# Regrouping the MLP tiles of an attention-plus-MLP kernel from 2,2,2,4,4,4,4,2 to 2,2,2,2,4,4,4,4, with the planner settings that go with it

## Chip, cores and metric

The kernel runs on one core of one Trainium2 chip. The metric is the device time of one execution in microseconds, the median over several. All times inside an execution are counted from the start of its profiled span. Engines carry the profile's names: PE (TensorE), DVE (VectorE), ACT (ScalarE), POOL (GpSimd), and SP (SyncE), which only issues transfers.

## What is computed

Windowed attention with four sink positions, followed by a two-layer MLP on the normalised result, with a residual. Cut to the essentials:

```python
# q, k, v: 4 batches x 8 heads x 768 positions x 64, float32; n_sink = 4, window = 128
scores = (q @ k.T) / 8
keep = (pos_k < 4) | ((0 <= pos_q - pos_k) & (pos_q - pos_k < 128))
a = softmax(where(keep, scores, -1e9)); attn = a @ v
x = attn.transpose(0, 2, 1, 3).reshape(4, 768, 512)
xn = (x - mean(x)) / sqrt(var(x) + 1e-6) * g_ln
out = x + relu(xn @ w_ch1) @ w_ch2          # 512 -> 2048 -> 512
```

## The kernel before, in words

**Tiles.** The 4 x 768 positions are 24 tiles of 128, numbered t = 6b + r (batch b, r from 0 to 5). A tile passes through these steps on PE:

- *scores* (function `scores`, line 625): eight matmuls of 64 rows, into two wide PSUM buffers. ACT takes the exponential (line 643). DVE (line 653; line 647 where r = 0) or POOL (lines 655 and 658) applies the window mask.
- *values* (function `values`, lines 713 and 716): the weighted sums of tile t use scores of tile t and of tile t - 1, and so come after the scores of t. For r of 2 and more there are also two sink matmuls (line 696). `normalise` follows on DVE: reciprocals and scaling (lines 752 and 753), statistics (765, 768), centring to `xn` (773).
- the *turn* of the centred tile into `xnt`, either on PE (line 812, copied back by ACT or DVE) or by a DMA transpose that SP issues (line 802) where t is in `BY_DMA`.
- *up* (line 836) and *down* (line 876). One `up` step fills one PSUM bank with 512 columns: for a group of four tiles it is 4 matmuls of 512 columns, for a group of two 8 of 256. `down` is 16 matmuls of 512 columns for a tile, then DVE's line 889, then SP's store (line 894).

**Groups.** `GROUPS` says how many consecutive tiles share an `up`. An up needs the turned `xnt` of *all* tiles of its group. The reciprocal standard deviation of a group is two POOL instructions (lines 785 and 787), emitted once for the group when its last tile's statistics exist.

**Sinks.** Per batch, `sinks` scores all queries against four keys (line 570). For batches 1 and 2 it is two parts: tiles of r = 2 and 3, then of r = 4 and 5. For the others it is one part over r = 2 to 5, so that it needs the transposed queries of four row blocks at once. A batch in `JOINED` has its first part appended behind the scores of its r = 2 tile.

**Values and scores.** Unless t - 1 is in `ALONE` (or t = 6), the values of tile t - 1 and the scores of tile t are one planned unit, in which the sink matmuls run on 64 rows for each half; a tile in `ALONE` has its values planned by themselves, with sink matmuls of 128 rows.

**Transfers.** For batches 1 to 3, POOL issues the loads: q and k blocks (line 409, into a ring of six `qb` buffers), v blocks (418), first rows of v (449). SP issues a DMA transpose for each `qb` (line 508) into `qkt`; when it has landed, its `qb` is free for the load six places later. POOL and SP take their instructions strictly in order, and so POOL's lines 785/787 and 655/658 stand in one queue with the loads, and SP's stores and turns in one queue with the transposes of q and k.

**Order.** `Plan.emit` is a list scheduler that runs when the kernel is built. Each operation has modelled costs, a due key, and dependences. A tile's attention key is `up_pos` of its group minus `LEAD` (30.0) minus 6.9 for each tile that follows it in the group. `up_pos` and `down_pos` count MLP work in the order `mlp_order`: ups of the first `NB0` = 3 groups, their downs, then up and down of each further group. DMA transposes carry a modelled extra latency, the last argument of `op`. The order is fixed in the program; on the chip each engine runs its list and waits where it must.

Of the kernel before, what the change touches and what calls it, by code (L numbers as in the profile page):

```python
# [38 lines left out]
class Plan:  # L39
# [18 lines left out]
    def op(self, engs, fn, deps=(), key=0.0, alloc=(), uses=(), lat=0.0):  # L58
        o = Op(engs, fn, deps, key, alloc, uses)
        o.lat = lat  # L60
        self.ops.append(o)
        return o
# [108 lines left out]
def kernel(  # L171
# [22 lines left out]
    NT = B * RB  # L194
# [4 lines left out]
    assert NS == 4 and W == 128 and D == 64 and S == 768 and DM == H * D  # L199


    GROUPS = [2, 2, 2, 4, 4, 4, 4, 2]
    JOINED = (3,)
    QB = 6
    ALONE = (6, 7, 8, 9)
    NB0 = 3
    NG = len(GROUPS)
    FIRST = [sum(GROUPS[:g]) for g in range(NG)]
    assert sum(GROUPS) == NT
    where = {FIRST[g] + i: (g, i) for g in range(NG) for i in range(GROUPS[g])}  # L210

# [19 lines left out]
    def copy(e, dst, src):  # L231
        if e == "ACT":
            nc.scalar.copy(dst, src)  # L233
        else:
            ENG[e].tensor_copy(dst, src)
# [7 lines left out]
    def room_for(buf):  # L243
        return wide[buf.slot // 2] if buf.pool == "pw" else single[buf.slot - 4]
# [5 lines left out]
    op = plan.op  # L250
# [4 lines left out]
    for s, g in mlp_order:  # L255
        (up_pos if s == "u" else down_pos)[g] = pos
        pos += 3.46 * GROUPS[g]
    LEAD = 30.0
    NEG_TILES = 3
    BY_DMA = [t for t in range(10, NT) if t != 13]  # L260
    W2_FIRST = 3

    def akey(t):
        g, ti = where[t]
        if g < NB0:
            return t - 100.0
        return up_pos[g] - LEAD - 6.9 * (GROUPS[g] - 1 - ti)

# [134 lines left out]
    def load_qk(b, x, r, key, deps=()):  # L403

        qb = Buf("qb", QB)

        def go(_):
            qb.t = qbp.tile([128, H * D], BF16, name="qb")
            nc.gpsimd.dma_start(qb.t.rearrange("p (h d) -> p h d", h=H),  # L409
                                (q, k)[x][b, :, 128 * r:128 * (r + 1), :].rearrange("h p d -> p h d"))  # L410

        prep(b, x, r, load(0.9, 0.9, go, key, deps, [qb]), key, qb)
# [43 lines left out]
    prepped, kqb, turns = {}, {}, {}  # L456

    def qkt_buf(b):
        if b in kqb:
            return []  # L460
        kqb[b] = Buf("qkt", 2)
        return [kqb[b]]
# [37 lines left out]
    def prep(b, x, r, lo, key, qb):  # L500

        alloc = qkt_buf(b)
        kb = kqb[b]

        def go(_):
            if kb.t is None:
                kb.t = qkt.tile([128, 2, HP, S], BF16, name="qkt")
            nc.sync.dma_start_transpose(kb.t[:, x, :, 128 * r:128 * (r + 1)], qb.t)  # L508

        o = op({"SP": 1.25}, go, [lo], key, alloc, [kb, qb])  # L510
        prepped[(b, r, x)] = op({"DMA": 0.75}, None, [o], key, (), [kb, qb], 0.8)

    def ready(b, hps, klo, khi, qlo, qhi):

# [165 lines left out]
    xb, xnb, xtb, mvb, rsb, turned = {}, {}, {}, {}, {}, {}  # L680
    aggr = {}

    def values(t, key, joined=False, narrow=False):
# [50 lines left out]
        if joined:  # L734
            return Joined(mm, deps, banks, uses, cost, lambda o: normalise(t, key, o, banks, sums))
        normalise(t, key, op({"PE": cost}, mm, deps, key, banks, uses), banks, sums)

    def normalise(t, key, o, banks, sums):

        b, r = divmod(t, RB)  # L740
        g, ti = where[t]
        vread[(b, r)] = o

        rc = {}

        def recip(_):
            xb[t].t = xpool.tile([128, H, D], BF16, name="xt")
            if len(banks) == 2:
                for half in range(2):
                    pv = sums[half].rearrange("p (h d) -> p h d", d=D + 1)  # L750
                    rc[half] = small.tile([128, 4], FP32, name=f"rc{half}")
                    nc.vector.reciprocal(rc[half], pv[:, :, D])  # L752
                    nc.vector.tensor_tensor(xb[t].t[:, 4 * half:4 * half + 4], pv[:, :, 0:D],  # L753
                                            rc[half].unsqueeze(2).to_broadcast([128, 4, D]), op=ALU.mult)
                return
            pv = room_for(banks[0])[:, :, 0:4 * (D + 1)].rearrange("p a (h d) -> p a h d", d=D + 1)
            rc[0] = small.tile([128, 2, 4], FP32, name="rc")
            nc.vector.reciprocal(rc[0], pv[:, :, :, D])
            nc.vector.tensor_tensor(xb[t].t.rearrange("p (a h) d -> p a h d", a=2), pv[:, :, :, 0:D],
                                    rc[0].unsqueeze(3).to_broadcast([128, 2, 4, D]), op=ALU.mult)  # L760

        def stat(_):
            xf = xb[t].t.rearrange("p h d -> p (h d)")
            st = small.tile([128, 6], FP32, name="st")
            nc.vector.bn_stats(st, xf)  # L765
            if g not in mvb:
                mvb[g] = small.tile([128, 4, 2], FP32, name="mv")
            nc.vector.bn_aggr(mvb[g][:, ti, :], st)

        def cen(_):  # L770
            xf = xb[t].t.rearrange("p h d -> p (h d)")
            xnb[t].t = xnpool.tile([128, DM], BF16, name="xn")
            nc.vector.scalar_tensor_tensor(xnb[t].t, in0=xf, scalar=mvb[g][:, ti, 0:1], in1=gb,  # L773
                                           op0=ALU.subtract, op1=ALU.mult)

        o = op({"DVE": 0.92 if len(banks) == 1 else 1.22}, recip, [o], key, [xb[t]], banks)
        o = op({"DVE": 0.9}, stat, [o], key, (), [xb[t]])
        aggr[t] = o
        o = op({"DVE": 0.75}, cen, [o, gb_done], key, [xnb[t]], [xb[t]])

        n = GROUPS[g]
        if ti == n - 1:
            def power(_):
                ve = small.tile([128, 4], FP32, name="ve")
                nc.gpsimd.tensor_scalar_add(ve[:, 0:n], mvb[g][:, 0:n, 1], 1e-6)
                rsb[g] = small.tile([128, 4], FP32, name="rs")
                nc.gpsimd.tensor_tensor(rsb[g][:, 0:n], ve[:, 0:n], neg_half[:, 0:n], op=ALU.pow)

            rs_done[g] = op({"POOL": 1.0}, power, [sinks_done] + [aggr[t - i] for i in range(n)], up_pos[g] + 15)

        alloc = []
        if ti == 0:
            xtb[g] = Buf("xnt", 3)
            alloc.append(xtb[g])

        def room():
            if xtb[g].t is None:
                xtb[g].t = xtpool.tile([128, NDM, 512], BF16, name="xnt")
            return xtb[g].t[:, :, 128 * ti:128 * (ti + 1)]

        if t in BY_DMA:
            o = op({"SP": 1.25}, lambda _: nc.sync.dma_start_transpose(room(), xnb[t].t), [o], key if t >= 10 else -50, alloc,
                   [xnb[t], xtb[g]])
            turned[t] = op({"DMA": 0.75}, None, [o], key, (), [xnb[t], xtb[g]], 1.0)
            return
        pt = Buf("pm", 0)

        def tr(_):
            room()
            pt.t = room_for(pt).bitcast(BF16)  # L810
            for j in range(NDM):
                nc.tensor.transpose(pt.t[:, 128 * j:128 * (j + 1)], xnb[t].t[:, 128 * j:128 * (j + 1)], ident)  # L812

        def back(e):
            copy(e, room(), pt.t[:, 0:512].rearrange("p (j c) -> p j c", j=NDM))

        o = op({"PE": 0.24}, tr, [o], key, alloc + [pt], [xnb[t], xtb[g]])
        turned[t] = op({"DVE": 0.69, "ACT": 0.59}, back, [o], key, (), [pt, xtb[g]])
# [84 lines left out]
    def attention(t, key):  # L903

        alone = t - 1 in ALONE
        trail = None
        if t % RB == 2:
            if t // RB in JOINED:
                trail = sinks(t // RB, key, True)
# [39 lines left out]
    for b in range(B):  # L949
# [34 lines left out]
        for r in range(RB):  # L984
            if b == B - 2:

                t = RB * (b + 1) + r
# [65 lines left out]
```

## Time and profile before

| | |
|---|---|
| median of 6 runs | 224.11 us (223.18 to 225.5) |
| profiled execution, device time | 223.18 us |
| its span, first to last instruction | 221.4 us |
| PE busy / weight loads busy | 213.9 us (97%) / 121.0 us (55%) |
| DVE, ACT, POOL busy | 115.1, 110.2, 92.0 us |
| granted PE clock | 1.00 throughout |
| PE waits in the span that the waits view names from 47 to 135 us | 1.3 us for `qkt` transposes, 1.0 us for a POOL mask |
| median time from issue to landing, 80 to 134 us | v 8.7, q 8.1, k 7.5, `qkt` transposes 7.8, `xnt` transposes 7.0 us |
| the same, 134 us to the end | `xnt` transposes 2.4, stores 2.0 us |

The profiled execution is the fastest of the six runs, 0.93 us below their median, and its device time is 1.78 us over its span. Matmuls overlap one another in the records, so that the busy share of PE says little about waits; the distance between the starts of successive matmuls does. The median time to landing shows two regimes: while the loads of batches 1 to 3 are under way a transfer lands 7 to 9 us after its issue, afterwards some 2 us after it.

### The profile page before, as it was taken

What the parts mean: (1) busy time and instruction counts of PE and PEld (TensorE: products, weight loads), DVE (VectorE), ACT (ScalarE), POOL (GpSimd) and SP (SyncE); (2) the same over time, 40 slices, a digit from 0 to 9 for tenths busy, and PEclk for the clock granted to TensorE, in tenths of its full rate; (3) what the DMA queues carried; (4) which work ended last, traced back from release to release, by engine and by line L of the source; (5) the groups of instructions that cost most, each with busy time, mean ns of one, the idle gap of its engine ahead of it and who ended that gap; (6) DMA issues with size and microseconds to landing.
All of it is one profiled execution on the core that took longest, in us unless ns stands there. A gap on an engine that the chain in (4) does not pass through costs nothing.

```text
span 221.4 us, 4388 instructions
## 1 busy us (share of the span) xinstructions
PE 213.9 (97%) x1728; PEld 121.0 (55%) x1728; DVE 115.1 (52%) x247; ACT 110.2 (50%) x159; POOL 92.0 (42%) x126
## 2 busy tenths in 40 slices
PE   7999999999989999999989999999999999999994
PEld 7465889874545554445535445544454544444853
DVE  5566867205888984486878675470017660021011
ACT  3679775555555187841376754066703266400620
POOL 8995634867625589469384621120005020000000
PEclk9999999999999999999999999999999999999999
DMA  6999999999999999999999992311011230012102
GB/s 165 169 192 199 190 207 188 117 154 193 165 146 241 161 209 155 132 156 178 136 196 173 144 168 74 118 47 24 4 47 47 71 87 11 0 51 94 47 0 95
DMA packets 104421, 27.41 MB, mean 124 GB/s; under 512 B 96081, under 2 KB 101457, under 8 KB 104402
## 3 DMA queue, kind: packets, MB, share of 16 engines
q0 software_dynamic: 73056, 13.64, 81.9%
q1 hardware_dynamic: 30802, 13.12, 30.8%
q10 hardware_dynamic: 544, 0.39, 0.5%
q8 instruction: 13, 0.21, 0.4%
q14 instruction: 6, 0.05, 0.1%
HBM read 28.05 MB, written 6.29 MB: 155 GB/s over the span
## 4 chain that ended last, share of the span: by engine, by line
PE 48%; DMA 32%; POOL 9%; issue 4%; ACT 3%; DVE 2%; SPq 1%; POOLq 0%; DVEq 0%
PE single L876 23%; PE single L836 20%; DMA qkt<-qb 10%; DMA w2s<-in_moe_w_ch_dram 7%; DMA qb<-in_k_dram 5%; DMA qb<-in_q_dram 4%; DMA qkn<-in_k_dram 3%; DMA vn<-in_v_dram 3%; POOL qb L409 2%; POOL qkn L371 2%; ACT e L643 2%; PE wide L625 2%; POOL vn L418 1%; SPq L508 1%; PE single L713 1%
## 5 line engine op out<-in xcount | busy, mean ns | idle before, releaser
L836 PE MATMUL single<-xnt,w1s 128*128 128x256 bf16 (+1 forms) x512 | 86.9, 326 | 0.0
L836 PEld LDWEIGHTS <-w1s 128*128 128x128 bf16 x512 | 48.9, 98 | 33.6 <-issue 1.7
L643 ACT ACTIVATE e<-wide 128x1024 bf16<-128x1024 f32 x44 | 43.8, 1024 | 43.7 <-PE wide L625 43.5
L876 PE MATMUL single<-w2s,h1t 128*128 128x512 bf16 x256 | 57.5, 379 | 0.0
L889 DVE SCALAR_TENSOR_TENSOR ot<-single,rs,xt 128x512 f32<-128x512 f32 (+2 forms) x25 | 18.2, 729 | 64.0 <-PE single L876 63.5
L845 ACT ACTIVATE h1t<-single 128x512 bf16<-128x512 f32 x60 | 35.8, 597 | 17.3 <-PE single L836 15.9
L876 PEld LDWEIGHTS <-h1t 128*128 128x128 bf16 x256 | 24.4, 98 | 29.6 <-issue 1.3
L876 PE MATMUL single<-w2s,h1n 128*128 128x512 bf16 (+2 forms) x144 | 29.5, 356 | 0.0
L845 ACT ACTIVATE h1n<-single 128x512 bf16<-128x512 f32 x30 | 17.9, 597 | 23.0 <-PE single L836 23.0
L409 POOL DMA_DIRECT2D qb<-in_k_dram x18 | 16.1, 897 | 16.3 <-DMA qkt<-qb 15.1
L418 POOL DMA_DIRECT2D vn<-in_v_dram x24 | 21.4, 899 | 2.6 <-DMA w2s<-in_moe_w_ch_dram 1.6
L409 POOL DMA_DIRECT2D qb<-in_q_dram x18 | 15.9, 884 | 13.4 <-DMA qkt<-qb 6.1
L655 POOL TENSOR_SCALAR_AFFINE_SELECT e<-e 128x512 bf16<-128x512 bf16 x6 | 4.1, 688 | 38.3 <-ACT e L643 38.3
L876 PEld LDWEIGHTS <-h1n 128*128 128x128 bf16 x144 | 12.9, 98 | 12.6 <-issue 0.4
L653 DVE TENSOR_TENSOR e<-e,mask 128x1024 bf16<-128x1024 bf16 x26 | 17.4, 683 | 3.8 <-ACT e L643 3.5
L773 DVE SCALAR_TENSOR_TENSOR xn<-xt,mv,gb 128x512 bf16<-128x512 bf16 x24 | 18.2, 758 | 0.6
L765 DVE BATCH_NORM_STATS2 st<-xt 128x6 f32<-128x512 bf16 x24 | 16.5, 689 | 0.4
L752 DVE RECIPROCAL rc<-single 128x4 f32<-128x4 f32 x34 | 6.0, 177 | 18.9 <-PE single L696 8.5
L713 PEld LDWEIGHTS <-e 128*128 128x128 bf16 x192 | 13.0, 98 | 3.8 <-POOL e L655 1.5
L753 DVE TENSOR_TENSOR xt<-single,rc 128x256 bf16<-128x256 f32 x34 | 14.4, 424 | 1.2
L625 PE MATMUL wide<-qkt 64*128 64x256 bf16 (+1 forms) x192 | 14.4, 262 | 0.1
L233 ACT COPY xnt<-single 128x512 bf16<-128x512 bf16 x9 | 5.3, 590 | 12.8 <-PE single L812 12.8
(69 smaller groups left out, 166.1 us busy)
## 6 DMA issues: line engine op xcount, KB each, us to landing
out_dram<-ot SPq DMA_DIRECT2D x23, 256.0 KB, 2.7
vn<-in_v_dram POOLq DMA_DIRECT2D x24, 128.0 KB, 7.7
qb<-in_q_dram POOLq DMA_DIRECT2D x18, 128.0 KB, 6.6
qb<-in_k_dram POOLq DMA_DIRECT2D x18, 128.0 KB, 6.3
w1s<-in_moe_w_ch_dram POOLq DMA_DIRECT2D x4, 512.0 KB, 11.0
w2s<-in_moe_w_ch_dram POOLq DMA_DIRECT2D x4, 512.0 KB, 14.5
qkn<-in_q_dram POOLq DMA_DIRECT2D x3, 192.0 KB, 4.8
qkn<-in_k_dram POOLq DMA_DIRECT2D x3, 192.0 KB, 5.2
```

The costliest lines, as they stand in the source:

```text
L409: nc.gpsimd.dma_start(qb.t.rearrange("p (h d) -> p h d", h=H), (q, k)[x][b, :, 128 * r:128 * (r + 1), :].rearrange("h p d -> p h d"))
L418: nc.gpsimd.dma_start(vn_buf[b % 2][:, r, :, 0:D], v[b, :, 128 * r:128 * (r + 1), :].rearrange("h p d -> p h d"))
L625: nc.tensor.matmul(pb.t[:, h2, i], lhsT=kb.t[64 * h2:64 * (h2 + 1), 1, hp, 128 * r:128 * (r + 1)], rhs=kb.t[64 * h2:64 * (h2 + 1), 0, hp, ...
L643: nc.scalar.activation(eb.t, pb.t, AF.Exp, scale=scale)
L653: nc.vector.tensor_tensor(ev, ev, mask1[:, 0:n].unsqueeze(1).to_broadcast([128, m, n]), op=ALU.mult)
L713: nc.tensor.matmul(pv[:, hh, :], lhsT=weights_of(t, half, i, h2, 0), rhs=vn[:, r, h, 0:D + 1], start=fresh and hh == 0, stop=(r == 0), ski ...
L765: nc.vector.bn_stats(st, xf)
L773: nc.vector.scalar_tensor_tensor(xnb[t].t, in0=xf, scalar=mvb[g][:, ti, 0:1], in1=gb, op0=ALU.subtract, op1=ALU.mult)
L836: nc.tensor.matmul(pb.t[:, n * i:n * (i + 1)], lhsT=w1s[:, j, 128 * (h0 + i):128 * (h0 + i + 1)], rhs=xtb[g].t[:, j, 0:n], start=(j == 0), ...
L845: nc.scalar.activation(hb.t, pb.t, AF.Relu)
L876: nc.tensor.matmul(pb.t[:, 0:n], lhsT=hidden(g, ht, ti), rhs=w2s[:, ht, c0:c1], start=(ht == 0), stop=(ht == NH1 - 1))
L889: nc.vector.scalar_tensor_tensor(ob.t[:, 0:n], in0=pb.t[:, 0:n], scalar=rsb[g][:, ti:ti + 1], in1=xb[t].t.rearrange("p h d -> p (h d)")[:, ...
```

## The change

The last small group moves to the front, so that groups of two hold tiles 0 to 7 and groups of four hold tiles 8 to 23. Only tiles 6 and 7 keep values planned by themselves. The sinks of batch 3 are no longer appended to scores. Tiles 8 and 9 are turned by DMA and tiles 10 and 11 on PE; tile 13 is turned by DMA as well, so that `BY_DMA` has 14 tiles for 13. The modelled latency of both kinds of DMA transposes is 1.5 us where it was 0.8 and 1.0.

```diff
-    GROUPS = [2, 2, 2, 4, 4, 4, 4, 2]
-    JOINED = (3,)
+    GROUPS = [2, 2, 2, 2, 4, 4, 4, 4]
+    JOINED = ()
     QB = 6
-    ALONE = (6, 7, 8, 9)
+    ALONE = (6, 7)
     NB0 = 3
...
-    BY_DMA = [t for t in range(10, NT) if t != 13]
+    BY_DMA = [8, 9] + list(range(12, NT))
...
-        prepped[(b, r, x)] = op({"DMA": 0.75}, None, [o], key, (), [kb, qb], 0.8)
+        prepped[(b, r, x)] = op({"DMA": 0.75}, None, [o], key, (), [kb, qb], 1.5)
...
-            turned[t] = op({"DMA": 0.75}, None, [o], key, (), [xnb[t], xtb[g]], 1.0)
+            turned[t] = op({"DMA": 0.75}, None, [o], key, (), [xnb[t], xtb[g]], 1.5)
```

## Prediction

> **What bounds the kernel.** I read the page's engine table first, then the PE timeline and the waits of PE, the chain that ended last, and the queues of POOL and SP.
>
> ```profile
> PE 213.9 (97%) x1728; PEld 121.0 (55%) x1728; DVE 115.1 (52%) x247; ACT 110.2 (50%) x159; POOL 92.0 (42%) x126
> ```
>
> Busy PE overlaps itself, so I priced matmuls by the distance between starts. In the chain:
>
> ```profile
> 102.89 8.55 DMA qkt<-qb
> ...
> 146.19 13.81 PE single L836 x64
> ...
> 204.43 6.99 PE single L836 x64
> ```
>
> That is 13.81/64 = 0.216 us for 512 columns and 6.99/64 = 0.109 us for 256: proportional, so a group of two costs no more PE time per tile than a group of four. After about 135 us PE is gapless. Its waits after the first 47 us are few:
>
> ```profile
> 65.40 0.29 PE L570 MATMUL single<-qkt,ks 128*32 128x256 bf16 x4 [0.78 <-DMA qkt<-qb]
> ...
> 111.36 3.62 PE L836 MATMUL single<-xnt,w1s 128*128 128x512 bf16 x16
> 115.96 0.20 PE L713 MATMUL single<-vn,e 128*128 128x65 bf16 x1 [0.98 <-POOL e L655]
> ```
>
> Measured by starts, they are 0.68 us (sinks of tiles 8 and 9, at 54.4), 0.94 us (sinks of tiles 10 and 11, first line), 0.2 us at 67.2 and 1.14 us (values of tile 16, last line): 2.95 us in all. What can be won is about 3 us; what can be lost is whatever PE waits anew. Each wait comes out of the transfer machinery, which has two queues in strict order:
>
> ```profile
> 73.63 0.87 POOL L409 DMA_DIRECT2D qb<-in_q_dram  x1 [2.07 <-DMA qkt<-qb]
> 74.81 0.79 POOL L785 TENSOR_SCALAR ve<-mv 128x4 f32<-128x4 f32 x1 [0.31 <-DVE mv L768]
> 75.68 1.33 POOL L787 TENSOR_TENSOR rs<-ve,neg_half 128x4 f32<-128x4 f32 x1
> 77.30 0.96 POOL L409 DMA_DIRECT2D qb<-in_k_dram  x1 [0.29 <-issue]
> ...
> 81.91 5.26 POOL L418 DMA_DIRECT2D vn<-in_v_dram  x6
> ...
> 114.08 0.90 POOL L409 DMA_DIRECT2D qb<-in_q_dram  x1
> 114.96 0.94 POOL L655 TENSOR_SCALAR_AFFINE_SELECT e<-e 128x512 bf16<-128x512 bf16 x1
> ```
>
> The reader sees a reciprocal deviation holding up loads for 3 us (74.8 to 77.3), and a mask that waits behind a load (114.96). SP's side:
>
> ```profile
> 117.25 1.21 SPq L508 DMA_TRANSPOSE qkt<-qb  x1
> 118.55 1.34 SPq L802 DMA_TRANSPOSE xnt<-xn  x1
> 119.99 4.29 SPq L508 DMA_TRANSPOSE qkt<-qb  x3
> ```
>
> and between 80 and 134 us the issues view gives from issue to landing:
>
> ```profile
> qkt<-qb SPq DMA_TRANSPOSE x17, 7.8
> xnt<-xn SPq DMA_TRANSPOSE x8, 7.0
> ```
>
> **PE work.** The built programs agree on PE up to the first downs (47.74 us in the trace). The matmuls of ups and downs are the same in number and width. One PE turn fewer (10 for 11): 4 x 0.056 = -0.22 us. Tiles 8 and 9 get their sink matmuls in 64-row pairs: the trace starts such a pair 0.12 us apart from its successor, where two full ones take 0.22, so -0.2 us. The sinks of batch 3 as their own block bring two changes of row layout, about 0.1 us each as around every block of line 570: +0.2 us. Sum: -0.2 us.
>
> **The early waits.** In the new order the sinks of tiles 8 and 9 stand at the same PE time as before and need the same q block (landing 55.11 us): 0.65 us stays. The sinks of 10 and 11 come 3.4 us of work later, at 67.5 us; their transpose landed at 65.36. One store now stands ahead of it in SP's queue; it carries 256 KB, at the page's mean of 124 GB/s 2.1 us if nothing overlaps, so 65.4 to 67.5: just covered. Scores of tiles 8 to 13 stand 1.7 to 5.9 us of PE work later than before, so their transposes are no longer last. Saved: 0.94 + 0.2 = 1.1 us. The values of tile 16 stand 2.45 us of work later than before, and their POOL mask is ready at about 115.9 plus what POOL's queue slips: 1.14 us saved, less the slip beyond half a microsecond.
>
> **Where PE would be without new waits.** From 47.74 us to the first up of tiles 12 to 15, the order of the changed program puts 252 matmuls of 512 columns (54.4 us), 64 of 256 (7.0), 14 blocks of scores (12 x 0.44 + 2 x 0.22 = 5.7), 13 of values (7.3), sinks and PE turns (1.3): 75.7 us. Changes of row layout: 14 blocks of scores at 0.19 and four of sinks at 0.15, 3.2 us, less the 0.2 for tiles 8 and 9. With 0.65 us of wait PE arrives at 47.74 + 75.7 + 3.0 + 0.65 = 127.1 us. The same count on the order before gives 128.1 where the trace has 127.76, so I trust it to 0.4 us. From there on 88.0 us of matmuls remain, plus what the trace before has beside matmuls from the same stage to the end (93.64 us for 89.79 of matmuls: 3.85), plus 0.1: 91.95 us. With no new wait the span is 127.1 + 91.95 = 219.1 us, 2.3 below before.
>
> **What is late next.** Three things move.
>
> First, POOL. The reciprocal deviation of tiles 8 to 11 now stands after batch 2's last k load and ahead of its six v loads, and needs the statistics of tile 11. Counted back from the arrival at 127.1, values of tile 11 end on PE at about 81.3 us; 1.2 us of scaling, an up's relu that DVE takes (its matmuls end at 82.8, then 0.69) and 0.87 of statistics bring it to 84.4. Lines 785 and 787 take 0.8 + 1.3 and the gaps 0.5, so that the v loads start at 87.0 for 81.91 us. Waiting behind: six v loads, then all of batch 3. The chain gives a v load 6.88 us from issue to landing at 81.91, queued behind others; behind an emptied queue the nearest row is the 3.1 us minimum of a `qkt` transpose. So 3.8 of the 5.1 us come back; of the rest the queue recovers part, since two `xnt` transposes of 86 to 91 us are gone from there and two stores come in. For batch 3 I take a slip of 1 us, with 0 and 3 as ends. Values of tile 12 need the first v block at 92.1 us; it lands by 87.0 + 3.1 to 6.9 = 90.1 to 93.9: I take nothing, as the queue has emptied; at worst 1.8 us.
>
> Second, the mask of tile 17 is now POOL's. It stands behind the masks of tile 16, two loads (0.9 each) and lines 785/787 of tiles 12 to 15 (up to 0.8 + 1.3). From 115.96 (when the mask begun at 114.96 let PE go) + 0.5 + 1.8 + 1.3 to 2.1 + 0.95 + 1 of slip it is ready at 121.5 to 122.3; PE wants it at 119.7. Cost 1.8 to 2.6 us, which moves the arrival of 127.1 to 128.9 to 129.7.
>
> Third, the first up of tiles 12 to 15 needs tile 15's turn. SP issues it after batch 3's second k transpose, a store, the fifth q transpose and the fourth k transpose. By the SP rows, the k load landed at 117.24, then 1.21 + 0.5 + 1.21 + 1.3 us: 121.75, with the slip 122.75 us. At 7.8 us, the row of the transposes around it, it lands at 130.55; at 7.0, 129.75; at 8.55, 131.3. In the order before, the first ups of this stage waited for nothing, since tiles 14 to 17 were wanted only at 146 us.
>
> The Trainium skill, page "DMA: Bandwidth & Descriptors", section "Anatomy of one DMA", puts a transfer issued by GpSimd at about 2.0 us plus its bytes over 436 GB/s, 2.3 us for 128 KB. The rows say 7 to 9 us until 134 us, and 2.4 us for the same transpose afterwards. By the page's figure, an estimate carried over to SP, the turn would land at 125.1 us and this wait would not exist. The row decides, as the transfer is issued into the crowded stage.
>
> PE thus starts these ups at 130.55, not at 129.7: the span is 130.55 + 91.95 = 222.5 us, 1.1 over before. The tile 17 wait lies inside that. On the median: 224.11 + 1.1 = 225.2 us. Later steps are covered: the sinks of batch 3 come 4.3 us of work later, for a q transpose issued some 2.5 us after the turn; tiles 16 to 23 are turned 20 us and more before their ups; the last tile is cut as before, so the tail stays. DVE is busy 23.4 of the 34.6 us from 111.4 to 146.
>
> **Rivals.** *A, the turn arrives in time.* Up to that turn the new order has one store (256 KB) fewer and one transpose more than the old, and if the slip is 0 and the queue shorter, it lands before 129. Then tile 17's mask ends last, or nothing: span 219.1 to 221.0, median 221.8 to 223.7. For it: the lighter queue; against it: the transfers that SP issued from 113.67 to 119.99 us took 6.7 to 8.3 us each.
>
> *B, POOL's hold is not recovered.* Batch 3 slips by 3 us or more, the turn lands at 132.5 to 133.5, and masks of tiles 16 and 17 wait too: span 224.5 to 225.5, median 227.2 to 228.2. It decides once batch 3's first k load (95.32 us) is issued after 98. For it: five loads in the trace wait for landings in turn, and the ring of six hands on a delay; against it: the seven transfers in flight at 81.91.
>
> *C, the waits move but weigh the same.* One of the two new waits is absorbed, 2.3 us saved and about as much lost: median 223.4 to 224.6.
>
> **How the numbers follow.** Chances: forecast 0.42 (224.6 to 226.3 us, by landings of 130.0 to 131.7), A 0.23, B 0.20, C 0.15. A measurement of this kernel can tell about 0.5%, 1.1 us, from no change: 223.0 to 225.2. Faster takes most of A, 0.20. C, the rest of A and under half of the forecast lie within: 0.33. The upper part of the forecast, B and an unnamed new wait: 0.47. The range of 8 in 10 is 222.3 to 227.8. The likeliest case's own is 224.6 to 226.3.
>
> **What would show it.** Right: no PE wait at the sinks of tiles 10 and 11; POOL's line 785 of tiles 8 to 11 near 85 us with the v loads behind it; a PE wait of 1 to 2 us on POOL at tile 17's values near 120 us; a wait of 1 to 2 us on an `xnt` transpose at the first 512-column ups of tiles 12 to 15 near 129 us; no gap after 135 us. Wrong: that up starting before 128.5 us (A), a PE wait before 100 us that is not the 0.65 of tile 8's sinks, or SP blocked by a store whose line 889 is late.

## The result, and the profile after

| | before | after |
|---|---|---|
| median | 224.74 us (37 runs) | 222.58 us (16 runs) |
| profiled execution | 223.18 us | 222.49 us |
| its span | 221.4 us | 220.7 us |

The ratio is 0.9925, with a 95% interval of 0.9899 to 0.9951: 0.75% or 1.7 us faster, where 225.2 us had been forecast, with 0.80 on "the same" or "slower". The ratio is formed from fast executions alone and so shows less than the 2.2 us between the medians. Two later sets of the same changed kernel gave 0.9975 (0.9941 to 1.001) and 0.9958 (0.9921 to 0.9994). The gain is thus 0.25 to 0.75%, near the limit of what can be told from no change.

The shares of the chain that ended last, before:

```profile
PE 48%; DMA 32%; POOL 9%; issue 4%; ACT 3%; DVE 2%; SPq 1%; POOLq 0%; DVEq 0%
```

The page of the changed kernel, the engine table and the shares of the chain:

```profile
PE 212.8 (96%) x1724; PEld 120.0 (54%) x1724; DVE 115.2 (52%) x247; ACT 108.5 (49%) x156; POOL 94.2 (43%) x129
...
PE 73%; DMA 14%; POOL 4%; DVE 3%; ACT 2%; issue 1%; ACTq 0%; DVEq 0%
```

PE is 73% of the chain that ended last, in place of 48%. Less of the end is set by transfers. The waits view of PE (total, times, longest) and the timeline of PE name what is left between 47 and 135 us:

```profile
PE single L570 <- DMA qkt<-qb: 2.1, 1, 2.1
...
PE single L713 <- POOL e L655: 0.3, 1, 0.3
```

```profile
56.70 0.29 PE L570 MATMUL single<-qkt,ks 128*32 128x256 bf16 x4 [2.09 <-DMA qkt<-qb]
...
128.91 4.26 PE L836 MATMUL single<-xnt,w1s 128*128 128x512 bf16 x19
```

The first line is the sinks of tiles 8 and 9. By starts that wait is 2.25 us, and the one for tile 17's mask 0.46 us: 2.71 us in all. The waits at the sinks of tiles 10 and 11 and at the values of tile 16 are gone. The second line is the first 512-column up of tiles 12 to 15. It bears no wait, and this is where the forecast had PE standing until 130.55 us. Only the weight load ahead of it stood still for a moment, for the turn of tile 15:

```profile
128.80 0.42 PEld L836 LDWEIGHTS <-w1s 128*128 128x128 bf16 x3 [0.22 <-DMA xnt<-xn]
```

So that turn landed just before 128.80 us, some 0.1 us before it would have cost time. Batch 3's first and third k load in POOL's timeline before, and the same timeline of the changed kernel:

```profile
95.32 0.87 POOL L409 DMA_DIRECT2D qb<-in_k_dram  x1 [0.86 <-DMA vn<-in_v_dram]
...
108.04 0.96 POOL L409 DMA_DIRECT2D qb<-in_k_dram  x1 [2.53 <-DMA qkt<-qb]
```

```profile
86.33 0.57 POOL L785 TENSOR_SCALAR ve<-mv 128x4 f32<-128x4 f32 x1 [1.58 <-DVE mv L768]
86.98 1.39 POOL L787 TENSOR_TENSOR rs<-ve,neg_half 128x4 f32<-128x4 f32 x1
88.34 5.35 POOL L418 DMA_DIRECT2D vn<-in_v_dram  x6
...
98.44 0.90 POOL L409 DMA_DIRECT2D qb<-in_k_dram  x1
...
108.24 0.88 POOL L409 DMA_DIRECT2D qb<-in_k_dram  x1 [1.45 <-DMA qkt<-qb]
...
120.44 1.08 POOL L655 TENSOR_SCALAR_AFFINE_SELECT e<-e 128x1024 bf16<-128x1024 bf16 x1
```

The hold is there: the v loads start at 88.34 us (forecast 87.0, before 81.91), and batch 3's first k load at 98.44 us (before 95.32, and past the 98 us from which rival B was to decide). But the third k load of batch 3 goes at 108.24 us against 108.04 before: of 3.1 us of delay 0.2 us is left after 10 us, since both kernels wait there for a place in the ring (1.45 and 2.53 us). These times differ between executions: a second profile of the kernel before (below) has its v loads at 83.88 us and the two k loads at 98.07 and 109.37 us, so that the sign of 98 us does not tell the kernels apart. SP's timeline shows what comes of it, and the issues view from 80 to 134 us (median from issue to landing) how:

```profile
114.11 2.67 SPq L508 DMA_TRANSPOSE qkt<-qb  x2
116.87 0.53 SPq L894 DMA_DIRECT2D out_dram<-ot  x1
117.89 2.77 SPq L508 DMA_TRANSPOSE qkt<-qb  x2
120.76 1.27 SPq L802 DMA_TRANSPOSE xnt<-xn  x1
```

```profile
vn<-in_v_dram POOLq DMA_DIRECT2D x12, 128.0 KB, 6.5
...
qkt<-qb SPq DMA_TRANSPOSE x18, 6.6
...
xnt<-xn SPq DMA_TRANSPOSE x8, 5.9
```

The turn of tile 15 is the transpose at 120.76 us, 2.0 us before the forecast's 122.75. By these medians every kind of transfer in this stage lands sooner than before, where the rows said 8.7, 7.8 and 7.0 us (behind 112 us the kernels no longer differ: `qkt` transposes issued from 112 to 124 us took 7.5 and 8.0 us in two profiles before, 8.3, 7.4 and 7.7 us in three after). That third k load landed 7.3 us after its issue, at 115.56, and before 9.2 us after it, at 117.24.

### The profile page after: what moved, and what is told of

Read it like the earlier page. It is cut to its first block, busy times and chain, and to the rows that moved or that the text cites. A ratio compares the mean times of both kernels' runs of the same rounds, so it can differ in the third digit from the quotient of the medians.

```text
span 220.7 us, 4388 instructions
## 1 busy us (share of the span) xinstructions
PE 212.8 (96%) x1724; PEld 120.0 (54%) x1724; DVE 115.2 (52%) x247; ACT 108.5 (49%) x156; POOL 94.2 (43%) x129
## 4 chain that ended last, share of the span: by engine, by line
PE 73%; DMA 14%; POOL 4%; DVE 3%; ACT 2%; issue 1%; ACTq 0%; DVEq 0%
PE single L876 32%; PE single L836 29%; DMA w2s<-in_moe_w_ch_dram 7%; PE wide L625 4%; DMA qb<-in_q_dram 3%; DMA qkt<-qb 3%; DMA xnt<-in_q_dram 2%; PE single L713 2%; PE single L716 1%; ACT e L643 1%; PE single L696 1%; PE wide L621 1%; DVE st L765 1%; POOL qb L409 1%; POOL rs L787 1%
## 5 line engine op out<-in xcount | busy, mean ns | idle before, releaser
L876 PE MATMUL single<-w2s,h1t 128*128 128x512 bf16 (+2 forms) x272 | 57.0, 367 | 0.0
L845 ACT ACTIVATE h1t<-single 128x512 bf16<-128x512 f32 x59 | 35.2, 597 | 34.1 <-PE single L836 33.6
L876 PEld LDWEIGHTS <-h1t 128*128 128x128 bf16 x272 | 25.6, 98 | 29.2 <-issue 0.8
L876 PE MATMUL single<-w2s,h1n 128*128 128x512 bf16 x128 | 29.6, 379 | 0.0
L845 ACT ACTIVATE h1n<-single 128x512 bf16<-128x512 f32 x29 | 17.3, 597 | 9.1 <-PE single L836 9.0
L773 DVE SCALAR_TENSOR_TENSOR xn<-xt,mv,gb 128x512 bf16<-128x512 bf16 x24 | 18.8, 785 | 0.6
L876 PEld LDWEIGHTS <-h1n 128*128 128x128 bf16 x128 | 11.9, 98 | 13.0 <-issue 0.4
L653 DVE TENSOR_TENSOR e<-e,mask 128x1024 bf16<-128x1024 bf16 x24 | 16.2, 682 | 3.5 <-ACT e L643 3.2
L655 POOL TENSOR_SCALAR_AFFINE_SELECT e<-e 128x512 bf16<-128x512 bf16 (+1 forms) x8 | 5.5, 693 | 24.3 <-ACT e L643 24.3
L713 PEld LDWEIGHTS <-e 128*128 128x128 bf16 x192 | 12.9, 98 | 3.0 <-POOL e L655 0.8
L716 PEld LDWEIGHTS <-e 128*128 128x128 bf16 x160 | 10.7, 97 | 1.4
```

Source lines behind the costliest of these rows:

```text
L653: nc.vector.tensor_tensor(ev, ev, mask1[:, 0:n].unsqueeze(1).to_broadcast([128, m, n]), op=ALU.mult)
L713: nc.tensor.matmul(pv[:, hh, :], lhsT=weights_of(t, half, i, h2, 0), rhs=vn[:, r, h, 0:D + 1], start=fresh and hh == 0, stop=(r == 0), ski ...
L845: nc.scalar.activation(hb.t, pb.t, AF.Relu)
L876: nc.tensor.matmul(pb.t[:, 0:n], lhsT=hidden(g, ht, ti), rhs=w2s[:, ht, c0:c1], start=(ht == 0), stop=(ht == NH1 - 1))
```

## Experiments

Waits below are extra distances between the starts of successive matmuls, as in the prediction. Matmul records that are missing from some profiles are not counted as waits. Ratios are to the kernel before on the same chip, with 95% intervals.

### Was the price of the third wait right? Tile 15's turn, later or not by DMA

SP issues the turn one or two places later (the last argument is 2 in `turn15_behind_2`; `in_turn`, left out here, holds tile 15's turn back for so many places of SP's list). All other orders stay as they are.

```diff
-                o.fn(e)
+                in_turn(o, e, 1)
...
```

Control:

> The changed kernel once more, as the control for the other three on this chip. Its two earlier sets gave 222.58 and 223.04 us and ratios of 0.9925 and 0.9975. Expected: 222.3 to 223.2 us, ratio 0.992 to 0.998; PE waits 0.8 to 2.3 us at the sinks of tiles 8 and 9, none at the first 512-column ups of tiles 12 to 15.

> The changed kernel with tile 15's DMA turn issued one place later by SP, behind the store that followed it; every other order unchanged. The store can go at about 120.8 us (line 889 of its tile ends at 120.34), so the turn is issued near 121.4 in place of 120.76. Theory M (the turn lands 7.5 to 8.1 us after its issue, and PE, which comes at 128.9, has no margin): it lands at 128.9 to 129.5, a wait of 0 to 0.6 us on an xnt transpose at the first 512-column ups, 0 to 0.5 us more than the control. Theory A (landings are set by the load on the queue and not by the issue, so that a place in the queue is worth nothing): no such wait, same time as the control within 0.3 us.

> The changed kernel with tile 15's DMA turn issued two places later by SP, behind the store and the sixth q transpose of batch 3, which went at 124.07 us when its load had landed; every other order unchanged. The turn is then issued near 125.4 us, later than the 122.75 of the forecast. Theory M (landing 7.4 to 7.8 us after the issue, and PE has nothing else to do at 128.9): it lands at 132.8 to 133.2, PE waits 3.8 to 4.3 us on an xnt transpose there, nothing absorbs it up to the end, time 226.2 to 227.2 us, ratio 1.007 to 1.016; had it been issued at 122.75 the wait would by the same rate have been 1.3 to 1.7 us, the forecast's. Theory A (part is absorbed, because later waits or the crowded queue ease while PE stands): the wait is under 3 us or the time rises by under 2.5 us over the control.

Control: 223.07 us, 0.9958 (0.9921 to 0.9994); waits of 0.43 us (sinks of tiles 8 and 9), 0.51 (values of tile 12, on a v load) and 1.79 (tile 17's mask), and 0.26 at the first 512-column ups, where none had been expected: the turn was issued at 121.19 us, and the weight load of these ups stood for it until 129.57 us.

One place later: 223.20 us, 0.9924 (0.9893 to 0.9956). The chain of this kernel, and its waits view:

```profile
121.26 7.88 DMA xnt<-xn
```

```profile
PE single L836 <- DMA xnt<-xn: 0.4, 1, 0.4
```

By starts the wait is 0.56 us, within theory M's 0 to 0.6. But the turn went only 0.07 us later than in the control, so this run says little.

Two places later: 224.66 us, 1.0005 (0.9977 to 1.0033). SP's timeline and the chain:

```profile
121.15 0.55 SPq L894 DMA_DIRECT2D out_dram<-ot  x1
121.89 2.02 SPq L508 DMA_TRANSPOSE qkt<-qb  x1
123.96 2.63 SPq L802 DMA_TRANSPOSE xnt<-xn  x2
```

```profile
123.96 7.21 DMA xnt<-xn
131.17 0.05 issue
131.22 4.49 PE single L836 x20
```

The turn landed 7.21 us after its issue, the ups began as it landed, and the span is 131.22 + 91.8 = 223.0 us; the forecast's tail was 91.95. So one transpose, two places later in a queue, costs 1.6 us (224.66 less 223.07) and undoes the gain of the change. The wait is 1.58 us and not the 3.8 to 4.3 expected, because the turn went at 123.96 us in place of 125.4, landed in 7.21 us in place of 7.4 to 7.8, and PE came at 129.6 in place of 128.9. A wait under 3 us had been put down as theory A's sign, yet nothing is absorbed: the wait is landing less arrival, and the span is 1.6 us over the control's 221.4. The mechanism and the price per microsecond of the forecast hold; its issue time did not. In the changed kernel the turn has no margin: issued at 120.76, 120.89 and 121.19 us in three profiles, it lets the weight load go at 128.80, 128.44 and 129.57 us, and the ups begin without a wait, 0.04 us late and 0.26 us late.

With tile 15 turned on PE:

```diff
-    BY_DMA = [8, 9] + list(range(12, NT))
+    BY_DMA = [8, 9] + [t for t in range(12, NT) if t != 15]
```

> The changed kernel with tile 15 turned on PE, so that the first ups of tiles 12 to 15 wait for no late transpose. Theory of the prediction (the DMA turn of tile 15 is on the path or a hair from it): 0.5 to 1.5 us below the changed kernel. Theory in time (it lands by 128.9 us, before PE asks): 0.2 us of PE work more and nothing saved, within 0.5 us of the changed kernel.

223.23 us, 0.9952 (0.9913 to 0.9992). The profile has one wait, 1.12 us at the sinks of tiles 8 and 9, in a span of 219.3 us. The time does not differ from the changed kernel's three medians (222.58 to 223.07 us), as theory "in time" had it: there is little to save on a turn that lands within 0.3 us of the moment it is wanted.

### Does POOL's hold cost anything?

POOL's reciprocal deviation of tiles 8 to 11 is made to wait for the last load issued at that point of the program, so that it stands behind batch 2's v loads.

```diff
-            rs_done[g] = op({"POOL": 1.0}, power, [sinks_done] + [aggr[t - i] for i in range(n)], up_pos[g] + 15)
+            rs_done[g] = op({"POOL": 1.0}, power, [sinks_done] + [aggr[t - i] for i in range(n)] + ([issued[-1]] if t == 11 else []), up_pos[g] + 15)
```

> The changed kernel, with POOL's reciprocal deviation of tiles 8 to 11 made to stand behind batch 2's v loads in place of ahead of them; PE's, ACT's and SP's orders as changed. Theory H (the hold of POOL is made good by the empty queue, as the fourth k block of batch 3 landed no later than in the kernel before): the v loads start near 82 us in place of 88.3, batch 3's first k load before 97 us in place of 98.4, but the time stays within 0.3% of the changed kernel, 222.0 to 223.3 us, ratio 0.990 to 0.997, and the wait at tile 17's mask (0.4 to 1.9 us) stays. Theory L (the late start of batch 3 is what makes the masks of tiles 16 and 17 late, and the sinks of batch 3 tight): no PE wait at 115 to 125 us, span 0.5 to 1.5 us below the changed kernel's, 221.0 to 222.0 us, ratio 0.986 to 0.990. Downs of tiles 8 to 11 need that deviation only behind 90 us; should DVE's line 889 wait for it, PE would show it at about 100 us and the time would rise by up to 1 us.

223.90 us, 0.9967 (0.9931 to 1.0002). Its POOL timeline:

```profile
85.64 0.87 POOL L409 DMA_DIRECT2D qb<-in_k_dram  x1 [3.04 <-DMA qkt<-qb]
86.51 5.26 POOL L418 DMA_DIRECT2D vn<-in_v_dram  x6
...
97.39 0.88 POOL L409 DMA_DIRECT2D qb<-in_k_dram  x1
...
113.21 0.79 POOL L785 TENSOR_SCALAR ve<-mv 128x4 f32<-128x4 f32 x1
114.08 1.04 POOL L787 TENSOR_TENSOR rs<-ve,neg_half 128x4 f32<-128x4 f32 x1
...
117.80 0.88 POOL L655 TENSOR_SCALAR_AFFINE_SELECT e<-e 128x512 bf16<-128x512 bf16 x1
```

With the hold gone, the v loads start at 86.51 us, not near 82. The k load ahead of them waits 3.04 us for a place in the ring of six, that is, for a transpose to land. Of the 6.4 us by which the v loads start later in the first profile after than in the first before, the hold was about 1.8. Batch 3's first k load goes at 97.39 us (97.87 to 98.44 in three profiles of the changed kernel), yet tile 15's turn is issued at 121.79 us, 0.6 to 1.0 us *later* than there. In this one profile a small lead at the start of the stage does not reach its end. The pair itself now stands at 113.2 us, ahead of the masks of tiles 16 and 17, and both are late:

```profile
PE single L713 <- POOL e L655: 3.5, 2, 1.8
```

Theory L's forecast fails, but the pair in its new place can make the masks late by itself, so that this run does not test whether the start of the loads does. H has the ratio right (0.990 to 0.997) and misses the time (222.0 to 223.3 us) and the v loads: nothing is won by moving the hold, and its profile has more waits at masks. The landings stay short (v 6.7, `qkt` 6.7 us), so it isn't the hold that shortens them.

### Which part of the change carries it?

Regrouping undone in the changed kernel, and the regrouping alone in the kernel before:

```diff
-    GROUPS = [2, 2, 2, 2, 4, 4, 4, 4]
+    GROUPS = [2, 2, 2, 4, 4, 4, 4, 2]
```

> The changed kernel with the old groups 2,2,2,4,4,4,4,2, all else as changed. Theory groups (the gain comes from asking for tiles 8 and 9 later and for the load chain of batches 1 and 2 less tightly): ratio to before 0.998 to 1.003, the gain is gone, with PE waits of 2.5 us or more after 47 us. Theory lead (the gain comes from the larger modelled latency of transposes, which puts what needs them later): 0.991 to 0.995, the gain stays.

> The kernel before with the new groups 2,2,2,2,4,4,4,4 alone. Theory groups: 0.993 to 0.996, two thirds of the gain or more. Theory lead: 0.998 to 1.003, no gain.

Undone: 231.54 us, 1.0363 (1.0308 to 1.0418). Its waits view, and a table of stretches (length, busy time of PE, PEld, DVE, ACT, POOL with instructions, granted PE clock, DMA share, GB/s):

```profile
PE single L836 <- DMA xnt<-xn: 4.1, 1, 4.1
PE single L713 <- DVE e L653: 3.1, 2, 2.2
```

```profile
73.00:84.00 11.00, 3.81 (x60) 2.35 (x58) 10.17 (x24) 4.31 (x5) 5.67 (x7) 0.79 1.77 172
84.00:90.00 6.00, 5.48 (x17) 2.23 (x19) 0.10 (x1) 1.56 (x3) 5.83 (x7) 0.54 1.84 184
```

With the old groups, tiles 8 and 9, which are turned by DMA, belong to the fourth group together with 6 and 7, and its first up waits 4.1 us for them. After the waits the granted clock is 0.54, about half.

Regrouping alone: 225.66 us, 1.0100 (1.0037 to 1.0163), with waits of 1.05, 0.39, 1.37 and 1.21 us between 53 and 69 us, all on `qkt` transposes, and a granted clock of 0.51 from 70 to 73 us. Both theories miss both runs: the regrouping alone gains nothing, and taking it back loses far more than the gain.

The old choice of tiles turned by DMA in the changed kernel:

```diff
-    BY_DMA = [8, 9] + list(range(12, NT))
+    BY_DMA = [t for t in range(10, NT) if t != 13]
```

> The changed kernel with the old list of DMA turns (10 to 23 but 13): tiles 10 and 11, the last of the first group of four, turned by DMA; 8, 9 and 13 on PE. Theory last tile (a DMA turn of the last tile of a group that is wanted at once takes 5 to 8 us where a PE turn and copy take about 1): a PE wait of 2 us or more on an xnt transpose at the first 512-column ups, 225 to 229 us. Theory indifferent (turns are covered): within 0.7 us of the changed kernel.

231.41 us, 1.0269 (1.0196 to 1.0341), above the 225 to 229 us of theory "last tile". Tiles 10 and 11 are then turned by DMA just ahead of their own ups:

```profile
PE single L836 <- DMA xnt<-xn: 6.2, 1, 6.2
```

SP issues the turn of tile 11 here, landing at 101.12 us for ups that PE is ready for at 95.0 us:

```profile
93.76 1.49 SPq L802 DMA_TRANSPOSE xnt<-xn  x1
```

The regrouping alone turns tiles 10 and 11 by DMA as well, and its first 512-column ups wait for nothing:

```profile
89.91 1.22 SPq L802 DMA_TRANSPOSE xnt<-xn  x1
```

There the turn lands at 95.02 us and the ups begin at 96.91. So it is not the groups and the list alone that make these turns late. The two kernels differ in the other three parts of the change, with which the turn of tile 11 is issued 3.9 us later and PE is ready 1.9 us earlier; which of them does it was not tried. These three, undone one at a time in the changed kernel:

```diff
-    ALONE = (6, 7)
+    ALONE = (6, 7, 8, 9)
```

> The changed kernel with values of tiles 6 to 9 planned by themselves, as before. PE work 0.2 us more; scores of tile 8 and 9 stand 2.7 and 4.3 us of work earlier, the sinks of tiles 10 and 11 2.2 us later. Theory order (scores earlier means waits for their transposes): a new PE wait of 0.5 us or more at scores of tiles 8 to 10, 0.5 to 2 us slower than the changed kernel. Theory indifferent: within 0.5 us.

```diff
-    JOINED = ()
+    JOINED = (3,)
```

> The changed kernel with the sinks of batch 3 once more appended to the scores of tile 20; the rest as changed. Theory N (this part of the change does nothing that can be measured, since these sinks stand behind 120 us where transfers land in time): 222.0 to 223.3 us, ratio to the kernel before 0.990 to 0.997, no PE wait behind 122 us. Theory W (appended sinks need the q block of row block 5 of batch 3 earlier, and PE waits for that transpose): a wait of 0.5 to 2 us between 118 and 130 us, ratio 0.996 to 1.004.

```diff
-        prepped[(b, r, x)] = op({"DMA": 0.75}, None, [o], key, (), [kb, qb], 1.5)
+        prepped[(b, r, x)] = op({"DMA": 0.75}, None, [o], key, (), [kb, qb], 0.8)
...
-            turned[t] = op({"DMA": 0.75}, None, [o], key, (), [xnb[t], xtb[g]], 1.5)
+            turned[t] = op({"DMA": 0.75}, None, [o], key, (), [xnb[t], xtb[g]], 1.0)
```

> The changed kernel with the old modelled latencies of 0.8 and 1.0 us for the two kinds of transposes. Theory groups: 0.991 to 0.996, the gain stays. Theory lead: 0.998 to 1.003, the gain is gone, and the profile shows PE waits on transposes at scores or sinks of tiles 6 to 11 of 1.5 us or more in sum beyond those of the changed kernel.

They gave 222.97 us, 0.9954 (0.9921 to 0.9988); 222.69 us, 0.9927 (0.9887 to 0.9967); and 222.87 us, 0.9963 (0.9937 to 0.9989). None of them does anything by itself that can be measured. (The one profile with sinks joined has a mean granted clock of 0.559, so that its waits are not known.) With values of tiles 8 and 9 alone, the wait that theory "order" expects is there, 1.23 us at the scores at 68.05 us, but none at the sinks of tiles 8 and 9, and the time is the same. With the old lead PE waits 0.61 us for the turn of tile 15, which confirms how thin that margin is. How the small parts make up for the 1% that the regrouping alone loses was not taken apart further.

### Do the waits account for the time, and do they stay away?

A second profile of each kernel:

> The unchanged kernel before, profiled a second time. Theory S (the profile that the forecast was made from was a lucky one, because waits of PE near 53 to 68 us and the landing of transposes differ from run to run): the second profile has a span of 222 to 223.5 us, and its PE waits add to 4 to 6 us where the first had 2.95, with the additional time at scores or sinks that wait for qkt transposes between 50 and 80 us, or at the values of tile 16. Theory F (the first profile was typical and the 1.8 us between its time and the median is overhead outside the span): span 221.2 to 221.8 us and waits of 2.7 to 3.2 us.

> The changed kernel as it stands, to have a second profile and a ratio on the chip of its neighbours. Both theories: 0.990 to 0.996 of the kernel before, some 221 to 222.5 us. If the 2.1 us wait at the sinks of tiles 8 and 9 in the first profile is a wait that varies with the landing of one transpose, this profile shows another value there (0.3 to 2.5 us); if it is fixed by the order, it shows 2.1 again.

The kernel before: 224.24 us, span 222.4 us, and gaps at 63.5 (0.76), 64.6 (1.38) and 115.1 us (1.65), 3.8 us where its first profile had 2.95:

```profile
PE single L713 <- POOL e L655: 1.5, 1, 1.5
PE single L570 <- DMA qkt<-qb: 1.2, 1, 1.2
...
PE wide L625 <- DMA qkt<-qb: 0.6, 1, 0.6
```

The changed kernel: 223.03 us, span 220.3 us, one wait of 1.59 us at the sinks of tiles 8 and 9. Theory S holds, though with a little less of waits than its 4 to 6 us: the first profile of before was a good one. The set's ratio of 0.9975 lies outside the expected 0.990 to 0.996. The order is fixed, but the landings are not.

Then the waits one by one. Only the sinks of tiles 8 and 9 placed later:

```diff
-        prepped[(b, r, x)] = op({"DMA": 0.75}, None, [o], key, (), [kb, qb], 1.5)
+        prepped[(b, r, x)] = op({"DMA": 0.75}, None, [o], key, (), [kb, qb], 4.0 if (b, r, x) == (1, 3, 0) else 1.5)
```

> The changed kernel with a modelled latency of 4.0 us instead of 1.5 for one transpose alone (batch 1, q, row block 3), so that the sinks of tiles 8 and 9 stand 1.5 us of PE work later. Theory PE (PE is the bound, its 1.4 to 2.3 us wait at these sinks is on the path): the wait falls to under 0.8 us, the time is 1 to 2 us below the changed kernel, ratio to before 0.985 to 0.991. Theory chain (the chain of loads and transposes sets the time up to 130 us, PE waits elsewhere instead): within 0.4 us of the changed kernel, with a new PE wait of about the same size before 130 us.

223.89 us, 0.9979 (0.9948 to 1.0011). The wait is gone, and three others have come: 1.38 us at the values of tile 12, 0.53 and 1.88 at the masks of tiles 16 and 17.

```profile
PE single L713 <- POOL e L655: 2.1, 2, 1.7
PE single L713 <- DMA vn<-in_v_dram: 1.2, 1, 1.2
```

PE that comes earlier finds the next transfer or mask not ready, as theory "chain" has it, though the time is 0.8 us over the changed kernel's 223.07 where that theory allowed 0.4. With the sinks, POOL's pair and tile 17's mask relieved together:

```diff
...
-                    if b > 1 or r < 4 and not b:
+                    if t != 17 and (b > 1 or r < 4 and not b):
```

> The changed kernel with three edits, one for each wait of PE that its profiles still show: the modelled latency of the transpose of queries of batch 1, row block 3, is 4.0 us, so that the sinks of tiles 8 and 9 are placed later; POOL's reciprocal deviation of tiles 8 to 11 stands behind batch 2's v loads; tile 17's mask is DVE's alone. Theory R (the waits are separate, and each edit removes its own): no PE wait over 0.5 us, span 217.5 to 219.0 us, 219.8 to 221.3 us of time, ratio 0.980 to 0.987. Theory C (the transfers are one chain of loads, ring, transposes, and what one wait gives up the next takes, as when the sinks alone were placed later and the values of tile 12, and the masks of tiles 16 and 17, waited 3.8 us): 0.993 to 0.999, with 2 to 4 us of waits at other places between 60 and 125 us, named by the waits view as transposes or masks.

> The three edits of the relief run once more (sinks of tiles 8 and 9 placed later by a modelled latency of 4.0 us, POOL's reciprocal deviation of tiles 8 to 11 behind the v loads, tile 17's mask on DVE alone), head to head with the changed kernel. Theory R (the edits remove waits for good): its median is 0.4 us or more below the control's, 221.5 to 222.4 us, ratio 0.987 to 0.993, and its profile shows under 2 us of PE waits from 50 to 135 us. Theory C (what one wait gives up another takes): within 0.4 us of the control or above it, and 2 us or more of waits, elsewhere than in its first profile.

222.65 us, 0.9934 (0.9894 to 0.9974), and 222.94 us, 0.9900 (0.9852 to 0.9947). The profiles differ: the first has 1.4 us of waits in a span of 219.1 us, the second 1.36 us at tile 16's mask and 1.83 at the turn of tile 15 in 221.2 us. Against its control (223.07 us) the second set gains 0.13 us in the median where theory R asks for 0.4, and its waits are over 3 us where R asks for under 2; only its ratio, 0.9900 against the control's 0.9958, lies in R's range, with intervals that overlap. So theory R is not borne out. Last, everything that was seen to wait:

```diff
-                    if b > 1 or r < 4 and not b:
+                    if t not in (16, 17) and (b > 1 or r < 4 and not b):
...
-    BY_DMA = [8, 9] + list(range(12, NT))
+    BY_DMA = [8, 9] + [t for t in range(12, NT) if t != 15]
```

(`relief_all` has the edits to the sinks and to POOL's pair as well, `relief_ns` only these two.)

> The changed kernel with an edit against every wait that its profiles and those of the variants showed: masks of tiles 16 and 17 on DVE alone, the turn of tile 15 on PE, the sinks of tiles 8 and 9 placed later (modelled latency 4.0 us for that one transpose), and POOL's reciprocal deviation of tiles 8 to 11 behind batch 2's v loads. Theory W (the waits of PE account for the time: in ten profiles the span less these waits was 217.5 to 218.7 us): with under 1 us of waits the span is 218.0 to 219.3 us, plus about 0.25 us for the PE turn, the time 219.9 to 221.2 us, ratio 0.980 to 0.987, below the changed kernel's 222.6 to 223.1 by 1.5 us or more. Theory C (waits move on along the chain of loads and transposes): 2 us or more of waits at other places, named by the waits view, and 222.0 to 223.5 us, ratio 0.990 to 0.997.

> Only two of those edits: masks of tiles 16 and 17 on DVE, tile 15's turn on PE; POOL's order up to batch 3 and the place of the sinks of tiles 8 and 9 as in the changed kernel. Theory W: the wait at the sinks of tiles 8 and 9 stays at 0.4 to 2.3 us, the masks and the turn hold nobody, span 218.5 to 220.5 us, time 220.4 to 222.2 us, ratio 0.982 to 0.991. Theory C: DVE, which now has 1.4 us of masks more near 115 to 121 us, makes the centred tiles or the values late in place of POOL, with 1 us or more of waits on DVE there, 222.3 to 223.3 us, ratio 0.992 to 0.997.

221.12 us, 0.9920 (0.9895 to 0.9945), and 221.55 us, 0.9922 (0.9885 to 0.9958): the two lowest medians of the study, though their ratios don't separate them from the changed kernel, which didn't run on that chip. In the first, no wait from 47 us on is over 0.6 us by starts; they add to 1.16 us above 0.5 each, with a span of 219.3 us. The second kept 0.70 us at the sinks and 1.08 us on tile 12's v load, in 220.6 us. Theory W has the first set's time and span right (up to 221.2 and 219.3 us), but neither ratio (0.980 to 0.987 and 0.982 to 0.991).

Span less waits (those over 0.25 us, by starts), over the profiles that kept the full clock:

| profile | span | waits | difference |
|---|---|---|---|
| before, first and second | 221.4, 222.4 | 2.95, 3.8 | 218.5, 218.6 |
| after, three | 220.7, 220.3, 221.4 | 2.71, 1.59, 3.24 | 218.0, 218.7, 218.1 |
| turn one and two places later | 221.0, 223.0 | 3.07, 5.19 | 217.9, 217.8 |
| turn on PE | 219.3 | 1.12 | 218.2 |
| power later | 223.1 | 4.85 | 218.2 |
| old lead | 220.8 | 2.58 | 218.3 |
| sinks later | 222.4 | 4.12 | 218.3 |
| three edits, twice | 219.1, 221.2 | 1.41, 3.49 | 217.7, 217.7 |
| relief all, relief ns | 219.3, 220.6 | 1.16, 1.77 | 218.2, 218.8 |

The difference is 217.7 to 218.8 us while the waits go from 1.1 to 5.2 us. So most of what tells the spans of these kernels apart is the sum of the waits between 47 and 135 us; what is left, 1.1 us, and the 1.1 us between two profiles of one kernel are too much to rank kernels by one profile each.

## Why the prediction was wrong

*PE work and the path without waits: right.* The forecast's 219.1 us with 0.65 us of wait is 218.45 without; the three profiles of the changed kernel give 218.0, 218.7 and 218.1. From the first 512-column ups to the end the span is 220.7 - 128.9 = 91.8 us, forecast 91.95.

*The early waits: two right, one wrong.* The waits at the sinks of tiles 10 and 11 and at the values of tile 16 went, as forecast. The 0.65 us at the sinks of tiles 8 and 9 was taken as a constant. It measured 2.25, 1.59 and 0.43 us in three profiles of one program: it is one landing against one time, and the landing varies.

*POOL's hold: right in place, wrong in consequence.* The v loads went at 88.34 us (forecast 87.0) and batch 3's first k load 3.1 us later than in the profile that the forecast was made from, its upper end. **The step that failed** is the issue time of tile 15's turn, 122.75 us, and in it the slip of 1 us that was to be left of the hold. The count started from the k load that landed at 117.24 us before (batch 3's third, which the prediction calls the second), put 1 us of slip on it, and so had its transpose at 118.25 us and the turn 4.5 us later (the steps named add to 4.2 us; 0.3 us of the 121.75 is in none of them). The load was issued 0.2 us later than before, as the wait for the ring of six made up the slip, but landed 1.7 us *earlier*. Its transpose went at 115.58 us (the second of the pair at 114.11) and the turn 5.2 us after it, because the last two transposes ahead of the turn went as their loads landed, at 117.87 and 119.41 us. So the slip, +1 us in the sum, measured -1.7, and the turn was issued at 120.76, 120.89 and 121.19 us in three profiles in place of 122.75; in the first it landed at 128.8 us in place of 130.55. Two things went into the error. A delay at the first load of the stage was carried to the third, though the ring lies between. And the landing time of that load was carried over from the kernel before, 9.2 us, where it took 7.3; in three profiles after, it landed at 115.56 to 115.94 us, in two before at 117.24 and 119.31. In four profiles with the new order (three of the changed kernel, and the one with the hold moved) v loads land in 6.4 to 7.0 us and `qkt` transposes in 6.6 to 6.8; in two of the kernel before, in 8.7 to 9.4 and 7.6 to 7.8. The forecast had named two `xnt` transposes fewer at 86 to 91 us as a reason for a lighter queue and then not used it for the durations. Which of the moved transfers lightens it was not tried, so why the landings are shorter stays open.

*Landing and price of the turn: right.* In the three profiles of the changed kernel it lands about 8.0, 7.5 and 8.3 us after its issue, in the two runs that move it 7.88 and 7.21, against 7.8, and the wait falls in full on the end once it occurs. The estimate of 2.3 us that the prediction took from the Trainium skill, page "DMA: Bandwidth & Descriptors", section "Anatomy of one DMA", would have been off by some 5 us for this transfer; the row was the right choice. Rival A, with "the slip is 0 and the queue shorter", is what happened, and it stood at 0.23.

*Tile 17's mask: right in time, smaller in price.* It ended at 121.5 us, the forecast's lower end, and cost 0.46 us as PE arrived late from the sinks; in the control it cost 1.79, the forecast's own lower end. That PE reached the ups of tiles 12 to 15 at 128.9, as the forecast's sum without the turn has it, is owed to these two errors cancelling.

*The base: wrong by 0.8 us.* The 1.1 us were worked out in the span of the first profile before and added to the median of 224.11, with the profiled execution 0.93 us below it. That profile was a good one: the second, at 224.24 us, has 0.85 us more of waits and 1.0 us more of span. The changed kernel's profile is 0.1 us from its median. Of the miss of 2.6 us, 1.8 lie in the span (222.5 against 220.7) and 0.8 in the step from span to median.

## What to carry to other kernels

Where loads go round a ring and wait for each other's landings, a late start isn't a late end: count the slip at the block that is needed, and ask whether the change also lightens the queue that sets the landing times, before these are carried over. Take a wait on a transfer from several profiles, and treat it as a difference of two times with its spread. Waits follow one another along the chain, so that removing one hands PE earlier to the next; here removing one or three showed no time, and even the run with nearly all of them removed is not set apart from the changed kernel by its ratio. When tiles are grouped anew, choose anew which are turned by DMA, and look where SP then issues each turn: in the changed kernel, either with the other's old value was 3 to 4% slower, while the same new groups and old list with the other old settings lost 1%.

## What the hardware showed unexpectedly

After a wait of 1.88 us PE fell to half clock in one profile and not in two others. In the run with tiles 8 and 9 alone, PE's timeline and the table of stretches:

```profile
122.33 0.20 PE L713 MATMUL single<-vn,e 128*128 128x65 bf16 x1 [1.72 <-POOL e L655]
```

```profile
116.00:122.00 6.00, 4.39 (x40) 2.18 (x39) 4.96 (x10) 1.02 (x1) 5.84 (x8) 1.00 2.28 206
122.00:129.00 7.00, 6.67 (x44) 3.11 (x45) 3.71 (x9) 1.94 (x2) 2.09 (x3) 0.76 2.02 157
```

Eight matmuls of 512 columns from 123.8 to 127.2 us started 0.427 us apart in place of 0.216: 1.7 us lost on top of the wait, and with it the span of 223.1 us, less 3.44 of waits, comes to 218.0. The same wait of 1.88 us in the runs with the turn two places later and with the sinks of tiles 8 and 9 later left the clock at 1.00. The Trainium skill, page "TensorE: Matmul & The Clock Gate", section "HAM oscillation — how this bites in real kernels", gives the abstract rule "no PE-idle gaps >~3.4µs." Here the half clock followed a shorter gap, with one of 0.33 us some 5 us ahead of it, and not every time.
